# Tail inputs of superblocks 1 to 3 of a deep cross network: by a transposing load and on-chip DMAs in place of TensorE

## The chip, the cores and the metric

The kernel runs on one core of one Trainium2 chip. The metric is the device time of one execution in microseconds; before the change it is 129.14 us, the median of 3 runs (129.04 to 129.23). Profiles are taken in separate executions.

## The reference

Six cross layers over a batch of 4096 rows with 416 features, all in bf16:

```python
B, F, D, L = 4096, 26, 16, 6        # Din = F * D = 416
x = x0                              # [4096, 416]
for l in range(6):
    x = x0 * (x @ ws[l] + bs[l]) + x    # ws[l]: [416, 416]
```

The kernel uses another form of it: with x_l = x0 * s_l and s_0 = 1, s_(l+1) = x_l @ ws[l] + bs[l] + s_l. The products are summed up in PSUM over all layers, and the biases and the 1, summed beforehand, are added where x_l = x0 * s_l is taken out.

## The kernel before

**Tiles.** The batch is cut into four superblocks of 1024 rows (`SB`), each with two halves of 512 (`H`). Activations lie transposed: features on the partitions, batch rows along the free axis. The 416 features are three full chunks of 128 (`CH`) and a tail of 32 features (`DR`). The tail would use 32 partitions only, so it is folded: the superblock's 1024 rows are four groups of 256 (`G`), and group g lies on partitions 32g to 32g+31 (`quad(g)`). For each superblock s, `x0t_sb[:, s, 0, :]` holds the folded tail of x0 and `x0t_sb[:, s, 1, :]` the same with neighbouring quads exchanged (group g^1 on quad g), which `tail_rows` needs so that both halves of a bank can be fed from any quad. The tail of x_l (`xt_sb`) has the same two forms.

**One layer of one superblock.** TensorE does nine `main` steps for half 0 (three output chunks by three input chunks, four matmuls of 32 columns side by side in each), `tail_rows` (the contribution of the 32 tail features), `tail_outs` (the 32 tail outputs, from the full chunks), and nine `main` steps for half 1; every matmul is issued at line 260. VectorE takes each bank out, multiplied with x0 (`leave`, line 412). The tail goes another way: ScalarE adds the bias (`tail_halves`, line 422), GpSimd multiplies with x0's tail (`leave_tail`, line 435), and ScalarE and GpSimd make the exchanged copy (`swap`, lines 399 and 401). Layer l+1 needs that tail only in `tail_rows`, after the nine steps of half 0.

**Where x0's tail comes from.** For superblock 0 a matmul with the identity transposes it in the first layer (`tail_in(0)`), and ScalarE copies it out of PSUM (line 383). For superblocks 1 to 3 all the rows' last 32 columns are loaded in one DMA, `xtl1`, into `xtl_sb`: 24 pieces of 64 bytes per partition, 192 KB. In layer 2 of the superblock before, `tail_in(s+1)` transposes eight tiles of 128 rows on TensorE into the free half of the first tail bank, `keep_tail_in` copies them to `x0t_sb` on ScalarE (line 390), and in layers 3 and 4 ScalarE makes the exchanged copy in four pieces (line 399).

**Order of the work.** `Plan.add` takes the operations in program order for each engine and works out the semaphore waits from what they read and write; nothing is reordered. A DMA is issued by the queue it is added to. On SyncE (SP in the profile) these are, in order: the first rows and weights, `xtl0`, the transposed x0 of half of superblock 0, the weights of layers 1 to 5 with `xtl1` between layer 2's and layer 3's, the three transposing loads of x0's full chunks for superblocks 1 to 3 (`load_transposed`, line 205), the rows `xr` that the end of the kernel needs, and then for each finished superblock four transposing DMAs of the result (`transpose_block`, lines 452 and 457) and, one layer after the next superblock's first, its store (`store_block`, line 469). Plain loads are issued at line 187. The last layer of the last superblock is computed in row form and stored in six pieces (line 666).

Of the kernel before, what the change touches and what calls it, by code (L numbers as in the profile page):

```python
# [8 lines left out]
ACTF = mybir.ActivationFunctionType  # L9
# [109 lines left out]
def bass_standalone__dcn_v2_cross__recsys_kernel(  # L119
# [6 lines left out]
    B, D = x0.shape  # L126
    L = ws.shape[0]
    NC = 3
    DF = 128 * NC
    DR = D - DF  # L130
    assert DR == 32
    SB = 1024
    NS = B // SB
    H = SB // 2
    G = SB // 4
    JS = SB // 128
    NJ = B // 128
    T_BANK = (6, 7)
# [3 lines left out]
    with ExitStack() as es:  # L142

        def sb(name, shape, dt=BF16):
            return es.enter_context(nc.sbuf_tensor(name, shape, dt))
# [2 lines left out]
        wt_sb = sb("wt_sb", [128, L, D])  # L148
        wc_sb = sb("wc_sb", [128, L, 2, 128])
        xin_sb = sb("xin_sb", [128, 4, D])  # L150
        xtl_sb = sb("xtl_sb", [128, NJ, DR])
        xr_sb = sb("xr_sb", [128, JS, D])
        x0T_sb = sb("x0T_sb", [128, NC, B])
        x0t_sb = sb("x0t_sb", [128, NS, 2, G])
# [10 lines left out]
        ident = sb("ident", [128, 128])  # L165
# [6 lines left out]
        ps = es.enter_context(nc.psum_tensor("ps", [128, 8, 512], FP32))  # L172
        psT = ps.bitcast(BF16)

        x0_v = x0.rearrange("(j p) d -> p j d", p=128)
        out_v = out.rearrange("(j p) d -> p j d", p=128)
        P = Plan()

        def quad(q):
            return slice(32 * q, 32 * q + 32)  # L180
# [5 lines left out]
        def load(queue, dst, src, name, writes):  # L186
            P.add(queue, lambda e: e.dma_start(dst, src), writes=writes, dma=name)  # L187

        def load_main(l):
            load(  # L190
                "sync", w_sb[:, l, :, :], ws[l, 0:DF, :].rearrange("(k p) n -> p k n", p=128), "w%d" % l, [("w", l)]
            )

        def load_rows(queue, i):
            load(queue, xin_sb[:, 2 * i:2 * i + 2, :], x0_v[:, 2 * i:2 * i + 2, :], "xin%d" % i, [("xin", i)])
# [7 lines left out]
        def load_transposed(s, a, b):  # L203
            P.add(
                "sync", lambda e: e.dma_start_transpose(x0T_sb[:, :, s * SB + a:s * SB + b], x0[s * SB + a:s * SB + b, 0:DF]),  # L205
                writes=[("x0T", s, c, h) for c in CH for h in HALVES if a <= h * H < b], dma="x0T%d" % s,
            )

        load_rows("sync", 0)
        load_rows("scalar", 1)  # L210
        load_main(0)
# [5 lines left out]
        load_main(1)  # L217
        load_tail_weights(2, L, "wt2", ("sync",) * 4)
        load_main(2)
        load("sync", xtl_sb[:, JS:NJ, :], x0_v[:, JS:NJ, DF:D], "xtl1", [("xtl", 1)])  # L220
        load_main(3)
        load_main(4)
        load_main(5)
        for s in range(1, NS):
            load_transposed(s, 0, SB)
        load("sync", xr_sb[:, :, :], x0_v[:, (NS - 1) * JS:NJ, :], "xr", [("xr",)])


# [3 lines left out]
            reads=[("ones",)], writes=[("dummy",)],  # L232
# [3 lines left out]
                out=ident[:, :], in_=ones_sb[:, 0:128], pattern=[[-1, 128]],  # L236
# [6 lines left out]
                out=u_sb[:, :], in_=ones_sb[0:L + 1, 0:L], pattern=[[1, L]],  # L243
# [34 lines left out]
        def src_main(s, l):  # L278
            if l == 0:
                return x0T_sb, s * SB  # L280
            return xT_sb[:, l % 2], 0
# [77 lines left out]
                adds=[("ps", T_BANK[h]) for h in HALVES],  # L359
            )  # L360

        def tail_in(s):
            def fn(pe):
                for o in range(2 if s == 0 else 1):
                    for r in range(2):
                        for g in range(4):
                            j = 2 * (g ^ o) + r
                            src = xin_sb[:, j, DF:D] if s == 0 and j < 4 else xtl_sb[:, s * JS + j, :]
                            b, c = (7, o * G) if s == 0 else (T_BANK[0], G)
                            ins = mm(  # L370
                                pe, ps[quad(g), b, c + r * 128:c + (r + 1) * 128], src, ident[:, :],
                                s == 0 and o == 0 and r == 0, (0, 32 * g),
                            )
                return ins

            b = 7 if s == 0 else T_BANK[0]
            P.add(
                "tensor", fn, reads=[("ident",), ("xtl", 0 if s == 0 else 1)] + ([("xin", 0), ("xin", 1)] if s == 0 else []),
                adds=[("ps", b)],
            )  # L380
            if s == 0:
                P.add(
                    "scalar", lambda e: e.activation(
                        out=x0t_sb[:, s, :, :], in_=ps[:, 7, :].rearrange("p (o c) -> p o c", o=2), func=ACTF.Copy
                    ), reads=[("ps", 7)], writes=[("x0t", s), ("x0t", s, "swapped")],
                )

        def keep_tail_in(s):
            P.add(
                "scalar", lambda e: e.activation(out=x0t_sb[:, s, 0, :], in_=ps[:, T_BANK[0], G:2 * G], func=ACTF.Copy),  # L390
                reads=[("ps", T_BANK[0])], writes=[("x0t", s)],
            )
        def swap(tile, key, engines):
            for g, eng in enumerate(engines):
                if eng is None:
                    continue
                dst, src = tile[quad(g), 1, :], tile[quad(g ^ 1), 0, :]
                if eng == "scalar":
                    fn = lambda e, d=dst, s=src: e.activation(out=d, in_=s, func=ACTF.Copy)  # L399
                else:  # L400
                    fn = lambda e, d=dst, s=src: e.tensor_copy(out=d, in_=s)  # L401
                P.add(eng, fn, reads=[key], parts=[key + ("swapped",)], shifts=True)
# [74 lines left out]
        for i in range(2):  # L477
            for c in CH:
                b = HEAD_BANKS[i][c]
# [10 lines left out]
                dst, src = x0T_sb[:, c, i * 256:(i + 1) * 256], psT[:, b, 0:256]  # L490
                if c == 1:
                    P.add(
                        "scalar", lambda e, d=dst, s=src: e.activation(out=d, in_=s, func=ACTF.Copy),
                        reads=[("ps", b)], writes=[("x0Tp", c, i)],
                    )
                else:
                    P.add(
                        "vector", lambda e, d=dst, s=src: e.tensor_copy(out=d, in_=s),  # L498
                        reads=[("ps", b)], writes=[("x0Tp", c, i)],
# [28 lines left out]
        for s in range(NS):  # L528
            for l in range(L):
                ending = s == NS - 1 and l == L - 2  # L530
                if s == NS - 1 and l == L - 1:
                    break
                if s == 0 and l == 0:
                    for k in CH:
                        for m in CH:
                            main(s, l, 0, m, k)
                        if k == 0:
                            bias_sums()
                        if k == 1:
                            tail_in(0)  # L540
                    tail_outs(s, l, True)
                    tail_rows(s, l, False)
                    for c in CH:
                        leave(s, l, 0, c)
                else:
                    for m in CH:
                        for k in CH:
                            main(s, l, 0, m, k)
                    tail_rows(s, l, l == 0)
                    for c in CH:  # L550
                        leave(s, l, 0, c)
                    tail_outs(s, l, False)
                if l == 2 and s < NS - 1:
                    tail_in(s + 1)
                leave_tail(s, l, not ending)
                if l == 2 and s < NS - 1:
                    keep_tail_in(s + 1)
                if s == 0 and l == 0:
                    corner(2, L, "wt2")
                if l == 1 and s > 0:  # L560
                    store_block(s - 1)
                if s < NS - 1 and l in (3, 4):
                    g = 2 * (l - 3)
                    swap(x0t_sb[:, s + 1], ("x0t", s + 1), tuple("scalar" if q // 2 == l - 3 else None for q in range(4)))
                if ending:
                    P.add(
                        "gpsimd", lambda e: e.tensor_tensor(
                            out=bt_sb[:, :], in0=cb_sb[:, NC, L - 1:L], in1=cb_sb[:, NC, L - 2:L - 1], op=ALU.subtract
                        ), reads=[("cb",)], writes=[("bt",)],
                    )  # L570
                    P.add(
                        "gpsimd", lambda e, t=t32_sb[:, l % 2, :]: e.tensor_scalar_add(st_sb[:, :], t, bt_sb[:, :]),
                        reads=[("t32", l % 2), ("bt",)], writes=[("st",)],
                    )
                    for c in CH:
                        keep_sum(0, c, "scalar")
                for m in CH:
                    for k in CH:
                        main(s, l, 1, m, k)
                    leave(s, l, 1, m)  # L580
                if ending:
                    for c in CH:
                        keep_sum(1, c, ("scalar", "scalar", "vector")[c])
            if s < NS - 1:
                transpose_block(s)


        s, l = NS - 1, L - 1
        ROW_BANKS = (6, 7, 0, 1, 2, 3, 4, 5)
        src, off = src_main(s, l)  # L590
# [126 lines left out]
```

## Time and profile before

| what | value |
|---|---|
| time, median of 3 runs | 129.14 us |
| time of the profiled execution | 130.38 us |
| its span | 129.1 us |
| TensorE (PE) busy | 124.2 us, 96% |
| VectorE (DVE) busy | 98.5 us, 76% |
| ScalarE (ACT) busy | 50.0 us, 39% |
| GpSimd (POOL) busy | 39.6 us, 31% |
| DMA, SP's queue | 33392 packets, 12.30 MB, 44.3% of 16 engines |
| granted TensorE clock | 1.00 |

The profile is one execution of the kernel, recorded by the hardware. The span runs from the first instruction to the last; the execution's time is a little longer than it. Busy time of an engine is the time in which at least one of its instructions ran; matmuls are pipelined, so PE being busy does not mean that it runs at its best. PEld is the loading of weights into TensorE, which goes on beside the matmuls. "SPq" and "ACTq" are the issuing of DMAs by those engines, and "to landing" is the time from the issue of a DMA to its last semaphore update. An arrow and a name in square brackets say how long the engine stood idle before a group and what ended that. The DMA engines are busy for most of the first 35 us, and in bursts afterwards.

### The profile page before, as it was taken

To read this page: it belongs to the slowest core of one execution; us is meant where nothing else is said; L and a number is where in the kernel's file an instruction comes from. 1 tells how busy PE (TensorE), PEld (TensorE's weight loads), DVE (VectorE), ACT (ScalarE), POOL (GpSimd) and SP (SyncE) were. 2 spreads that over 40 slices of the span, in tenths; PEclk is the share of its full clock that TensorE was granted. 3 is DMA by queue.
4 is the path that set the end of the run, shared out by engine and by line. 5 is a ranking of instruction groups with operands and counts; after the bars stand their busy time and mean duration, and the time that the engine had idled before them with its cause. 6 is when DMAs were issued, how large, how long until landed. Compare 5 with 4: busy or idle time off the path is not lost.

```text
span 129.1 us, 5328 instructions
## 1 busy us (share of the span) xinstructions
PE 124.2 (96%) x2424; PEld 64.5 (50%) x2424; DVE 98.5 (76%) x150; ACT 50.0 (39%) x112; POOL 39.6 (31%) x88
## 2 busy tenths in 40 slices
PE   6997999999999999999999999999999999999991
PEld 4543545545545545545545545455455455455660
DVE  0309588797797797797797797797797797797973
ACT  1525133473523242373422252364422252253920
POOL 6054342242222251241221350340320441440550
PEclk9999999999999999999999999999999999999999
DMA  3969779999809808000009407000009506100017
GB/s 97 280 147 240 86 209 285 172 197 168 259 9 194 68 8 265 7 0 5 0 5 183 86 0 244 25 5 0 5 0 149 120 5 211 58 0 5 0 38 231
DMA packets 34082, 13.12 MB, mean 102 GB/s; under 512 B 25350, under 2 KB 34060, under 8 KB 34060
## 3 DMA queue, kind: packets, MB, share of 16 engines
q1 hardware_dynamic: 33392, 12.30, 44.3%
q10 hardware_dynamic: 668, 0.48, 1.1%
q8 instruction: 19, 0.31, 1.1%
q14 instruction: 3, 0.02, 0.1%
HBM read 4.07 MB, written 3.41 MB: 58 GB/s over the span
## 4 chain that ended last, share of the span: by engine, by line
PE 88%; SPq 5%; DMA 4%; issue 0%; DVE 0%
PE ps L260 88%; DMA w_sb<-in_ws_dram 4%; SPq L187 3%; SPq L205 2%; DVE o_sb L648 0%
## 5 line engine op out<-in xcount | busy, mean ns | idle before, releaser
L412 DVE SCALAR_TENSOR_TENSOR xT_sb<-ps,cb_sb,x0T_sb 128x512 bf16<-128x512 f32 x120 | 80.9, 744 | 20.3 <-PE ps L260 20.3
L260 PE MATMUL ps<-xT_sb,w_sb 128*32 128x512 bf16 (+1 forms) x1596 | 84.6, 364 | 0.7 <-DMA w_sb<-in_ws_dram 0.7
L260 PEld LDWEIGHTS ps<-xT_sb,w_sb 128*32 128x32 bf16 x1596 | 40.7, 97 | 38.1 <-issue 4.0
L422 ACT ACTIVATE t_sb<-ps,cb_sb 64x256 f32<-64x256 f32 x46 | 21.6, 468 | 52.1 <-PE ps L260 51.8
L435 POOL TENSOR_TENSOR xt_sb<-t_sb,x0t_sb 128x256 bf16<-128x256 f32 x20 | 13.4, 672 | 63.5 <-ACT t_sb L422 63.5
L399 ACT ACTIVATE xt_sb<-xt_sb 32x256 bf16<-32x256 bf16 x38 | 15.7, 414 | 15.4 <-POOL xt_sb L435 15.2
L260 PE MATMUL ps<-x0T_sb,w_sb 128*32 128x512 bf16 (+1 forms) x336 | 19.1, 369 | 0.1
L401 POOL COPY xt_sb<-xt_sb 32x256 bf16<-32x256 bf16 x38 | 14.9, 392 | 2.4
L412 DVE SCALAR_TENSOR_TENSOR xo_sb<-ps,cb_sb,x0T_sb 128x512 bf16<-128x512 f32 x18 | 12.1, 744 | 2.5 <-PE ps L260 2.5
L260 PEld LDWEIGHTS ps<-x0T_sb,w_sb 128*32 128x32 bf16 x336 | 8.3, 97 | 8.1 <-issue 0.8
L260 PE MATMUL ps<-xt_sb,wt_sb 32*128 32x512 bf16 (+1 forms) x152 | 11.6, 326 | 0.0
L260 PE MATMUL ps<-xt_sb,wc_sb 32*128 32x256 bf16 x76 | 7.4, 268 | 0.0
L260 PEld LDWEIGHTS ps<-xt_sb,wt_sb 32*128 32x128 bf16 x152 | 2.3, 91 | 8.1 <-DVE xT_sb L412 6.4
L435 POOL TENSOR_TENSOR xot_sb<-t_sb,x0t_sb 128x256 bf16<-128x256 f32 x3 | 2.0, 673 | 9.9 <-ACT t_sb L422 9.9
L260 PE MATMUL ps<-w_sb,xT_sb 128*32 128x416 bf16 (+1 forms) x60 | 5.1, 339 | 0.0
L399 ACT ACTIVATE x0t_sb<-x0t_sb 32x256 bf16<-32x256 bf16 x12 | 4.9, 410 | 0.1
L253 POOL COPY wc_sb<-wt_sb 32x32 bf16<-32x32 bf16 (+1 forms) x12 | 2.8, 232 | 6.5 <-DMA wt_sb<-in_ws_dram 6.0
L648 DVE TENSOR_TENSOR o_sb<-ps,xr_sb 128x416 bf16<-128x416 f32 x6 | 3.4, 588 | 1.3 <-PE ps L260 1.0
L268 PE MATMUL ps<-ones_sb 128*128 128x256 bf16 x12 | 2.9, 419 | 1.2 <-DVE ones_sb L229 1.2
L260 PEld LDWEIGHTS ps<-xt_sb,wc_sb 32*128 32x128 bf16 x76 | 3.9, 93 | 0.3
L498 DVE COPY x0T_sb<-ps 128x256 bf16<-128x256 bf16 x4 | 1.2, 292 | 3.7 <-PE ps L483 3.4
L444 ACT ACTIVATE sS_sb<-ps,cb_sb 128x512 bf16<-128x512 f32 x5 | 3.0, 689 | 0.0
(41 smaller groups left out, 33.7 us busy)
## 6 DMA issues: line engine op xcount, KB each, us to landing
out_dram<-o_sb SPq DMA_DIRECT2D x3, 832.0 KB, 4.2
w_sb<-in_ws_dram SPq DMA_DIRECT2D x6, 312.0 KB, 5.2
xr_sb<-in_x_dram SPq DMA_DIRECT2D x1, 832.0 KB, 5.8
wt_sb<-in_ws_dram SPq DMA_DIRECT2D x4, 104.0 KB, 3.2
out_dram<-o_sb SPq DMA_DIRECT2D x2, 208.0 KB, 2.2
xin_sb<-in_x_dram ACTq DMA_DIRECT2D x1, 208.0 KB, 3.3
xin_sb<-in_x_dram SPq DMA_DIRECT2D x1, 208.0 KB, 3.0
out_dram<-o_sb ACTq DMA_DIRECT2D x2, 104.0 KB, 2.0
```

The source lines that it names most:

```text
L187: P.add(queue, lambda e: e.dma_start(dst, src), writes=writes, dma=name)
L205: "sync", lambda e: e.dma_start_transpose(x0T_sb[:, :, s * SB + a:s * SB + b], x0[s * SB + a:s * SB + b, 0:DF]),
L253: "gpsimd", lambda e, p=p, g=g: e.tensor_copy(out=wc_sb[p, a:b, g % 2, quad(g)], in_=wt_sb[p, a:b, DF:D]), reads=[("wt", name), ("wc", nam ...
L260: return pe.matmul(dst, lhsT=lhsT, rhs=rhs, start=start, stop=True, skip_group_check=True, tile_position=pos,)
L268: ins = pe.matmul(ps[:, 7, 0:256], lhsT=ones_sb[:, 0:128], rhs=ones_sb[:, :], start=True, stop=True)
L399: fn = lambda e, d=dst, s=src: e.activation(out=d, in_=s, func=ACTF.Copy)
L401: fn = lambda e, d=dst, s=src: e.tensor_copy(out=d, in_=s)
L412: "vector", lambda e: e.scalar_tensor_tensor(out=dst, in0=ps[:, bank(h, c), :], scalar=cb_sb[:, c, l:l + 1], in1=x0T_sb[:, c, o:o + H], op ...
L422: "scalar", lambda e, p=p, h=h: e.activation(out=dst[p, :], in_=ps[p, T_BANK[h], 0:G], func=ACTF.Identity, bias=cb_sb[p, NC, l:l + 1]), re ...
L435: "gpsimd", lambda e: e.tensor_tensor(out=dst, in0=t, in1=x0t_sb[:, s, 0, :], op=ALU.mult),
L444: fn = lambda e: e.activation(out=o, in_=i, func=ACTF.Identity, bias=b)
L648: "vector", lambda e: e.tensor_tensor(out=o_sb[:, jj, :], in0=ps[:, b, 0:D], in1=xr_sb[:, j, :], op=ALU.mult), reads=[("ps", b), ("xr",)], ...
```

## The change

`xtl_sb` shrinks to superblock 0, and the `xtl1` load goes. After each of the three `load_transposed(s, 0, SB)`, SP also issues `load_last_columns(s)`: a transposing DMA of the last 128 columns of the superblock's 1024 rows into `tT_sb[:, s - 1, :]`, so that the 32 tail features lie on partitions 96 to 127 and the rows along the free axis. `place_tail(s)` then issues, on SP too, eight DMAs from SBUF to SBUF of 32 partitions by 256 elements: for each of the two forms and each group, from partitions 96 to 127 to the quad where it belongs. They stand where ScalarE's `keep_tail_in` stood, in layer 2 of the superblock before; in SP's order that is behind `xr` for superblock 1, and behind the store of the last finished superblock for 2 and 3. `tail_in` is left for superblock 0 alone, `keep_tail_in` and the four swaps of `x0t_sb` in layers 3 and 4 are gone. `tail_rows` of layer 0 and `leave_tail` now wait for those DMAs.

```diff
-        xtl_sb = sb("xtl_sb", [128, NJ, DR])
+        xtl_sb = sb("xtl_sb", [128, JS, DR])
+        tT_sb = sb("tT_sb", [128, NS - 1, SB])
...
+        def load_last_columns(s):
+            P.add(
+                "sync", lambda e: e.dma_start_transpose(tT_sb[:, s - 1, :], x0[s * SB:(s + 1) * SB, D - 128:D]),
+                writes=[("tT", s)], dma="tT%d" % s,
+            )
+
+        def place_tail(s):
+            for o in range(2):
+                for g in range(4):
+                    dst, src = x0t_sb[quad(g), s, o, :], tT_sb[128 - DR:128, s - 1, (g ^ o) * G:((g ^ o) + 1) * G]
+                    P.add(
+                        "sync", lambda e, d=dst, r=src: e.dma_start(d, r), reads=[("tT", s)],
+                        writes=[("x0t", s), ("x0t", s, "swapped")], dma="x0t%d" % s,
+                    )
...
         load_main(2)
-        load("sync", xtl_sb[:, JS:NJ, :], x0_v[:, JS:NJ, DF:D], "xtl1", [("xtl", 1)])
         load_main(3)
         load_main(4)
         load_main(5)
         for s in range(1, NS):
             load_transposed(s, 0, SB)
+            load_last_columns(s)
         load("sync", xr_sb[:, :, :], x0_v[:, (NS - 1) * JS:NJ, :], "xr", [("xr",)])
...
-        def tail_in(s):
+        def tail_in():
             def fn(pe):
-                for o in range(2 if s == 0 else 1):
+                for o in range(2):
                     for r in range(2):
                         for g in range(4):
                             j = 2 * (g ^ o) + r
-                            src = xin_sb[:, j, DF:D] if s == 0 and j < 4 else xtl_sb[:, s * JS + j, :]
-                            b, c = (7, o * G) if s == 0 else (T_BANK[0], G)
+                            src = xin_sb[:, j, DF:D] if j < 4 else xtl_sb[:, j, :]
...
-        def keep_tail_in(s):
-            P.add(
-                "scalar", lambda e: e.activation(out=x0t_sb[:, s, 0, :], in_=ps[:, T_BANK[0], G:2 * G], func=ACTF.Copy),
-                reads=[("ps", T_BANK[0])], writes=[("x0t", s)],
-            )
...
-                if l == 2 and s < NS - 1:
-                    tail_in(s + 1)
                 leave_tail(s, l, not ending)
                 if l == 2 and s < NS - 1:
-                    keep_tail_in(s + 1)
+                    place_tail(s + 1)
...
-                if s < NS - 1 and l in (3, 4):
-                    g = 2 * (l - 3)
-                    swap(x0t_sb[:, s + 1], ("x0t", s + 1), tuple("scalar" if q // 2 == l - 3 else None for q in range(4)))
```

More of the change, by code (lines that the diff above doesn't have):

```diff
@@ L367, in fn @@
                             j = 2 * (g ^ o) + r
-                            src = xin_sb[:, j, DF:D] if s == 0 and j < 4 else xtl_sb[:, s * JS + j, :]
-                            b, c = (7, o * G) if s == 0 else (T_BANK[0], G)
+                            src = xin_sb[:, j, DF:D] if j < 4 else xtl_sb[:, j, :]
                             ins = mm(
-                                pe, ps[quad(g), b, c + r * 128:c + (r + 1) * 128], src, ident[:, :],
-                                s == 0 and o == 0 and r == 0, (0, 32 * g),
+                                pe, ps[quad(g), 7, o * G + r * 128:o * G + (r + 1) * 128], src, ident[:, :],
+                                o == 0 and r == 0, (0, 32 * g),
                             )
                 return ins
-            b = 7 if s == 0 else T_BANK[0]
+            P.add("tensor", fn, reads=[("ident",), ("xtl", 0), ("xin", 0), ("xin", 1)], adds=[("ps", 7)])
             P.add(
-                "tensor", fn, reads=[("ident",), ("xtl", 0 if s == 0 else 1)] + ([("xin", 0), ("xin", 1)] if s == 0 else []),
-                adds=[("ps", b)],
-            )
-            if s == 0:
-                P.add(
[L383 to L386, printed above, removed]
-        def keep_tail_in(s):
-            P.add(
-                "scalar", lambda e: e.activation(out=x0t_sb[:, s, 0, :], in_=ps[:, T_BANK[0], G:2 * G], func=ACTF.Copy),
-                reads=[("ps", T_BANK[0])], writes=[("x0t", s)],
+                "scalar", lambda e: e.activation(
+                    out=x0t_sb[:, 0, :, :], in_=ps[:, 7, :].rearrange("p (o c) -> p o c", o=2), func=ACTF.Copy
+                ), reads=[("ps", 7)], writes=[("x0t", 0), ("x0t", 0, "swapped")],
             )
@@ L539, in bass_standalone__dcn_v2_cross__recsys_kernel @@
                         if k == 1:
-                            tail_in(0)
+                            tail_in()
                     tail_outs(s, l, True)
```

## The prediction

> **What bounds the kernel now.** I read the page first, then the chain that ended last in order of time, then busy time by stretches cut at the layers, then SP's queue and the DMA table.
>
> From the page:
>
> ```profile
> span 129.1 us, 5328 instructions
> PE 124.2 (96%) x2424; PEld 64.5 (50%) x2424; DVE 98.5 (76%) x150; ACT 50.0 (39%) x112; POOL 39.6 (31%) x88
> ...
> PE 88%; SPq 5%; DMA 4%; issue 0%; DVE 0%
> ```
>
> The chain in order of time:
>
> ```profile
> 7.29 5.14 DMA w_sb<-in_ws_dram
> 12.43 0.04 issue
> 12.47 114.02 PE ps L260 x2184
> 126.49 0.02 issue
> 126.52 0.59 DVE o_sb L648
> ```
>
> From 12.47 us the chain is PE alone, without a break. Before that it is SP's issues and the load of the weights of layer 1. So PE work taken out between 12.47 and 126.49 shortens the run one for one, and anything else counts only if it makes PE wait.
>
> Stretches from one layer's tail_rows to the next (columns: stretch, its length, then busy us and instructions of PE, PEld, DVE, ACT, POOL, the clock, DMA share, GB/s). Superblocks 0, 1, 2; layer 2 and then layer 3 of each:
>
> ```profile
> 19.41:24.40 4.99, 4.99 (x109) 2.59 (x106) 4.04 (x6) 2.15 (x5) 1.45 (x3) 1.00 1.16 228
> 24.40:29.28 4.88, 4.88 (x102) 2.48 (x98) 4.04 (x6) 2.60 (x6) 1.45 (x3) 1.00 1.00 210
> 48.79:53.78 4.99, 4.99 (x109) 2.59 (x106) 4.05 (x6) 2.15 (x5) 1.46 (x3) 1.00 0.53 172
> 53.78:58.66 4.88, 4.88 (x102) 2.48 (x98) 4.04 (x6) 2.60 (x6) 1.45 (x3) 1.00 0.01 3
> 78.17:83.16 4.99, 4.99 (x109) 2.59 (x106) 4.04 (x6) 2.15 (x5) 1.46 (x3) 1.00 0.53 174
> 83.16:88.04 4.88, 4.88 (x102) 2.48 (x98) 4.04 (x6) 2.60 (x6) 1.45 (x3) 1.00 0.01 3
> ```
>
> A layer with the tail input in it is 0.11 us longer, three times alike, with DVE equally busy (4.04 of 4.99 or 4.88, so DVE is not the bound) and the clock at 1.00.
>
> The timeline inside the first of them, the place in superblock 1 that needs the tail, SP's queue, and four rows of DMA issues:
>
> ```profile
> 20.30 0.28 PE L260 MATMUL ps<-ident,xtl_sb 128*32 128x128 bf16 x8
> 23.30 0.38 ACT L390 ACTIVATE x0t_sb<-ps 128x256 bf16<-128x256 f32 x1
> ...
> 39.03 0.12 PEld L260 LDWEIGHTS ps<-x0t_sb,wt_sb 32*128 32x128 bf16 x8 [0.42 <-DVE xo_sb L412]
> ```
> ```profile
> 10.19 1.57 SPq L187 DMA_DIRECT2D xtl_sb<-in_x_dram  x1
> 11.80 5.89 SPq L187 DMA_DIRECT2D w_sb<-in_ws_dram  x3
> 17.74 11.63 SPq L205 DMA_TRANSPOSE x0T_sb<-in_x_dram  x3
> 29.42 0.59 SPq L187 DMA_DIRECT2D xr_sb<-in_x_dram  x1
> 37.37 4.12 SPq L452 DMA_TRANSPOSE o_sb<-xo_sb  x3
> ```
> ```profile
> xr_sb<-in_x_dram SPq DMA_DIRECT2D x1, 832.0 KB, 5.8
> wt_sb<-in_ws_dram SPq DMA_DIRECT2D x6, 26.0 KB, 2.2
> o_sb<-xo_sb SPq DMA_TRANSPOSE x9, 3.3
> ot_sb<-xot_sb SPq DMA_TRANSPOSE x3, 2.4
> ```
>
> The reader is to see 39.03 us: today's tail of superblock 1 is there by 33.7 (the last swap, 32.87 + 0.82), five us early. In the changed kernel it comes through SP's queue, behind everything of the second and third fence.
>
> **The change part by part.**
>
> *Off PE: 3 x 8 matmuls of 128 columns.* By the stretches: 4.99 - 4.88 = 0.11 each, 0.33 in all, on the path. It fits the single records: the eight start between 20.30 and 20.36 and the next matmul at 20.41. [...]
>
> *Off ACT: 3 copies of 0.38 and 12 swaps of 0.41 (4.9 by the page), 6.0 us of busy time.* Worth nothing: behind them ACT waits 1.8, 1.4 and 1.6 us for PE in the three layers of superblock 0 concerned. Were that cover gone, up to 0.85 a layer would come back as gain; no row asks for it. leave_tail of layer 2 no longer waits for the eight matmuls, 0.1 earlier; POOL then waits some 3 us for ACT in every layer anyhow.
>
> *Off SP and the DMA engines: the xtl1 load,* 1.57 us of SP at 10.19. The chain's load (w1) was issued at 7.29, ahead of it, so the 12.43 should stay; w3 to w5 come earlier and nobody waits for them. Bounds for w1: 0 to a gain of 0.66, PE's whole idle time there; I take 0. In the three weight issues behind it (5.89 us where 0.43 apiece is normal) up to 5.89 - 3 x 0.43 = 4.6 us of SP time may be freed too.
>
> *Onto SP: three transposing loads of 256 KB.* Nearest rows: o_sb transposes of the same 128 x 1024 took 4.12 / 3 = 1.37 of SP each; a third of an x0T load is 11.63 / 9 = 1.29. Three: 3.9 to 4.1 us. All stand before xr.
>
> *Onto SP: 8 placing DMAs of 16 KB per superblock.* Nearest row by size and partitions: the 26 KB wt loads, 0.42 to 0.57 of SP and 2.2 us to landing. 8 x 0.47 = 3.8 us. The first waits for its transposing load; queued behind it on SP are transpose_block and store_block. That load is issued about 20 us and, landing as late as the worst x0T (7.4 us), is there by 28, before SP comes to it.
>
> *When is the tail of superblock 1 there?* SP ends xr today at 30.01. Without xtl1, with three more loads, then the eight: 30.01 - 1.57 + 4.0 + 3.8 = 36.2 at the latest; 31.6 if all 4.6 us are freed; I take 34, in the middle, as the stall of the weight issues follows the slow xtl1 rows but not surely all of it. From the end of the last issue to landing 2.2 - 0.47 = 1.7: 33.3 to 37.9, middle 35.7. The DMA engines give a second bound, as the placing stands behind xr in one queue. xr lands at 29.42 + 5.8 = 35.2. Three loads by DMA time: 768 KB took about 3.8 us of the stretch that starts at 17.74, so 3 x 1.3 = 3.8 more; xtl1 occupied the engines from 12.4 to about 15.3 (88 GB/s there), 2.9 less; the eight add some 0.6. So 36.7, and 39.6 if the freed 2.9 us goes unused. I take 36.7. Needed at 39.03 - 0.11 = 38.9: 2.2 us to spare, 0.7 late at worst. Cost taken 0; ends 0 and 0.7.
>
> [...] The four 26 KB loads issued from 5.29 to 7.25 landed 2.0 us after their issues at the median, so they overlapped; I go by them.)
>
> *Superblocks 2 and 3.* The placing stands behind the out stores, at 48.5 and 77.9, ends 4 us later on a queue otherwise idle to 66.75 and 96.13, and is needed at about 68 and 97.5. Nothing.
>
> *The output transposes of block 0* need SP at 37.4; SP is free by 36.2 at the latest. Their cover if late: ot_sb lands at about 45.6, POOL copies it at 47.70: 2.1 us.
>
> *New waits on PE,* three times for a DMA semaphore in tail_rows of layer 0. Not shown before in that place; PEld's gap there is 0.42 whichever semaphore ended it. Bounds 0 and 0.1 each (a quarter of that gap); I take 0.
>
> **Sum.** -0.33 + 0 + 0. The profiled execution took 130.38, 1.28 more than its span; the unprofiled median is 129.14 and the PE stretches should be the same in it. 129.14 - 0.33 = 128.8, a span of 128.8 too. That is 0.26%; about 0.2% (0.26 us) is what a measurement can tell from no change here, so the forecast is just over it.
>
> **The rivals.**
>
> *The tail of superblock 1 comes late (slower).* Place: tail_rows of layer 0, superblock 1. For it: eight DMAs at the end of a queue that is full up to 35.2 today. Against: the 2.2 us. It decides from a landing after 38.9; at 39.26 the gain is gone, at 39.5 it is measurably slower. By the worst bound (39.6) it is 129.14 - 0.33 + 0.7 = 129.5; with one of the long pauses that the transposes had (ot_sb 4.0 against 2.3 us, another 1.7), 131.2.
>
> *The gain is eaten by waits (same).* Three PE waits at 0.1 each leave 0.03: 129.1. Against it: 4.88 us for layers that wait for ACT, DVE or POOL alike.
>
> *More than PE's part (faster).* w1 earlier without the xtl1 descriptors in the rings: at most 0.66 more, 128.15. Against it: xtl1 is issued 2.9 us after w1, behind it in each ring.
>
> **How the numbers follow.** No stall 0.71 (128.8, own range 128.65 to 129.0, the spread of the three times to both sides); late tail 0.19 (129.0 to 131); waits 0.06 (129.1); more 0.04. Faster by over 0.2%: four fifths of the first (its centre is close to the bound) and the last, 0.61. Same: the rest of the first (0.14), the waits and the mild end of the late tail (0.03), 0.23. Slower: the rest of the late tail, 0.16. The range runs from 128.6, below the likeliest by the spread, to 129.5, the worst landing by the bounds; about 0.05 lies below it and 0.1 above.
>
> **What would show it.** Layer 2 of superblocks 0 to 2 at 4.88; L390 and the x0t_sb form of L399 gone; xr issued between 27.7 and 32.5; the eight placing issues ending between 31.6 and 36.2; PE's chain 113.7 us from 12.47. Wrong, if PE or PEld waits for a DMA on x0t_sb near 39, if the w1 row moves, or if a placing DMA takes SP well over 0.5 us.

## The result

The changed kernel is slower: 134.73 us median of 6 executions (131.90 to 136.30) against 129.18 us (128.95 to 129.27). The ratio is 1.026, 95% interval 1.021 to 1.030, but it leaves out executions over 1.5% above the fastest, which here are the changed kernel's own long stalls, so the median belongs beside it. On another chip it took 134.12 to 136.16 us in four executions (ratio 1.042, 1.036 to 1.048). The forecast was 128.8, in a range of 128.6 to 129.5.

### The profile after

The page of the changed kernel, from an execution of 135.76 us (the line PEclk is the granted clock in tenths, in 40 slices):

```profile
span 134.5 us, 5290 instructions
PE 126.7 (94%) x2400; PEld 65.1 (48%) x2400; DVE 98.7 (73%) x150; ACT 44.3 (33%) x97; POOL 39.7 (29%) x88
...
PEclk9999999999995599999999999999999999999999
...
PE 67%; SPq 27%; DMA 2%; issue 1%; DVE 0%
```

PE's share of the chain fell from 88% to 67%: the chain no longer joins PE at 12.47. Its end, in order of time:

```profile
38.45 2.70 DMA x0t_sb<-tT_sb
41.15 0.14 issue
41.29 90.10 PE ps L276 x1664
131.39 0.02 issue
131.41 0.59 DVE o_sb L648
```

It runs through SP's queue up to the last of the eight placing DMAs of superblock 1, which lands at 41.15. In the timeline PE waits for it:

```profile
41.26 0.27 PEld L276 LDWEIGHTS ps<-x0t_sb,wt_sb 32*128 32x128 bf16 x8 [3.67 <-issue]
41.29 1.01 PE L276 MATMUL ps<-x0t_sb,wt_sb 32*128 32x512 bf16 x7 [3.21 <-DMA x0t_sb<-tT_sb]
```

The layers by stretches, in the columns of the prediction: layer 2 of superblock 0, then the last layer of superblock 0 with the stall at its end, the first of superblock 1, and the two next, of which the last is again a layer 2:

```profile
18.50:23.38 4.88, 4.88 (x101) 2.48 (x98) 4.04 (x6) 1.77 (x4) 1.46 (x3) 1.00 1.31 170
33.13:41.29 8.16, 4.95 (x101) 2.52 (x98) 4.04 (x6) 0.94 (x2) 0.67 (x1) 0.95 0.71 175
41.29:49.03 7.74, 7.74 (x97) 3.37 (x98) 4.32 (x6) 1.77 (x4) 1.45 (x3) 0.61 0.46 88
49.03:53.91 4.88, 4.88 (x101) 2.48 (x98) 4.04 (x6) 1.77 (x4) 1.85 (x4) 1.00 0.02 3
53.91:58.78 4.87, 4.87 (x100) 2.47 (x96) 4.04 (x6) 1.77 (x4) 1.46 (x3) 1.00 0.62 194
```

The reader is to see three things. Layer 2 is 4.88 and 4.87, the saving that was forecast. The layer before the tail's arrival is 8.16, 3.28 more than a layer. And the layer after it is 7.74 with PE busy throughout and the clock at 0.61: PE came back from the stall at half speed (a clock of 0.50 from 40.43 to 47.25). From the two rows, the time at half clock is 2 x (0.05 x 8.16 + 0.39 x 7.74) = 6.85 us.

SP's queue:

```profile
12.54 4.79 SPq L206 DMA_TRANSPOSE x0T_sb<-in_x_dram  x1
17.38 2.33 SPq L212 DMA_TRANSPOSE tT_sb<-in_x_dram  x1
19.75 5.53 SPq L206 DMA_TRANSPOSE x0T_sb<-in_x_dram  x1
25.32 1.30 SPq L212 DMA_TRANSPOSE tT_sb<-in_x_dram  x1
26.66 4.41 SPq L206 DMA_TRANSPOSE x0T_sb<-in_x_dram  x1
31.12 1.31 SPq L212 DMA_TRANSPOSE tT_sb<-in_x_dram  x1
32.47 0.58 SPq L188 DMA_DIRECT2D xr_sb<-in_x_dram  x1
33.10 5.95 SPq L221 DMA_DIRECT2D x0t_sb<-tT_sb  x8
39.09 4.06 SPq L457 DMA_TRANSPOSE o_sb<-xo_sb  x3
```

The two spans differ by 5.34 us (134.47 - 129.13): stall +3.28, half clock 7.74 - 4.88 = +2.86, three shorter layers -0.33, layer 1's weights, late in the execution shown of before and not here, -0.9 with the head, and the end of the kernel +0.4. That last one, which the prediction has nowhere, is read from the end of the chain: from 131.41 + 0.59 = 132.0 to the span's end it is 2.5 us, before it was 129.1 - 127.1 = 2.0.

### The profile page after: what moved, and what is told of

Read it like the earlier page. It is cut to its first block, busy times and chain, and to the rows that moved or that the text cites. A ratio compares the mean times of both kernels' runs of the same rounds, so it can differ in the third digit from the quotient of the medians.

```text
span 134.5 us, 5290 instructions
## 1 busy us (share of the span) xinstructions
PE 126.7 (94%) x2400; PEld 65.1 (48%) x2400; DVE 98.7 (73%) x150; ACT 44.3 (33%) x97; POOL 39.7 (29%) x88
## 3 DMA queue, kind: packets, MB, share of 16 engines
HBM read 3.87 MB, written 3.41 MB: 54 GB/s over the span
## 4 chain that ended last, share of the span: by engine, by line
PE 67%; SPq 27%; DMA 2%; issue 1%; DVE 0%
PE ps L276 67%; SPq L206 12%; SPq L188 7%; SPq L221 4%; SPq L212 4%; DMA x0t_sb<-tT_sb 2%; DVE o_sb L648 0%
## 5 line engine op out<-in xcount | busy, mean ns | idle before, releaser
L276 PE MATMUL ps<-x0T_sb,w_sb 128*32 128x512 bf16 (+1 forms) x336 | 21.4, 401 | 0.1
L404 ACT ACTIVATE xt_sb<-xt_sb 32x256 bf16<-32x256 bf16 x38 | 15.7, 414 | 15.5 <-POOL xt_sb L440 15.3
L276 PEld LDWEIGHTS ps<-x0T_sb,w_sb 128*32 128x32 bf16 x336 | 8.9, 104 | 9.6 <-issue 2.9
L276 PE MATMUL ps<-xt_sb,wt_sb 32*128 32x512 bf16 (+1 forms) x152 | 11.6, 326 | 0.0
L276 PE MATMUL ps<-x0t_sb,wt_sb 32*128 32x512 bf16 (+1 forms) x32 | 2.9, 371 | 3.2 <-DMA x0t_sb<-tT_sb 3.2
```

The costliest lines, as they stand in the source:

```text
L276: return pe.matmul(dst, lhsT=lhsT, rhs=rhs, start=start, stop=True, skip_group_check=True, tile_position=pos,)
```

## The experiments

Three questions: is the place in SP's queue the cause of the late tail; is the half clock the stall's doing; and what is left when both are gone. All edits are against the changed kernel unless it is said otherwise.

### Early placing of superblock 1

```diff
             load_transposed(s, 0, SB)
+            if s == 2:
+                place_tail(1)
             load_last_columns(s)
...
-                if l == 2 and s < NS - 1:
+                if l == 2 and 0 < s < NS - 1:
                     place_tail(s + 1)
```

> The changed kernel with the eight placing DMAs of superblock 1 issued right behind the second x0T load, ahead of two transposing loads, the third x0T load and xr. Theory (place in SP's queue): the tail landed at 41.15 because SP came to the first placing DMA at 33.10; here SP comes to it at about 25, the tail lands by 33, no stall at 37.7 and no halved clock: 3.3 + 2.9 us come back, about 128 to 128.9. Rival (the placing DMAs are slow by themselves or choke on the transposing loads around them): 0.6 to 1.2 us of SP each and a late last engine here too, landing after 38.8, a stall of 1 us or more and over 130.

129.96 us against 129.50; ratio 1.0033 (1.0009 to 1.0058). SP's queue and the two layers around the old stall, from its timeline and stretches:

```profile
24.71 5.86 SPq L221 DMA_DIRECT2D x0t_sb<-tT_sb  x8
```
```profile
33.42:38.30 4.88, 4.88 (x101) 2.48 (x98) 4.04 (x6) 0.94 (x2) 0.67 (x1) 1.00 1.16 182
38.30:43.18 4.88, 4.88 (x102) 2.48 (x98) 4.04 (x6) 1.77 (x4) 1.46 (x3) 1.00 1.42 266
```

Stall and half clock are gone, although the eight issues take as long as before (5.86 us). So the place in the queue decides. But the kernel is no faster than before. The 0.33 us of the layers is there: the unbroken last stretch of PE's chain is 116.63 us, against 116.95 in both profiles below that have the old way of the tail and no wait for layer 1's weights. It is given back elsewhere. The chain ends at 126.15 and its span is 128.6, 2.45 us later: the longer end is in this kernel too. The two make +0.1 us; the median is 0.46 higher, and the interval reaches down to +0.12. What the rest of the 0.46 is, no profile shows.

### The xr load behind the placing

```diff
-        load("sync", xr_sb[:, :, :], x0_v[:, (NS - 1) * JS:NJ, :], "xr", [("xr",)])
...
                     place_tail(s + 1)
+                    if s == 0:
+                        load("sync", xr_sb[:, :, :], x0_v[:, (NS - 1) * JS:NJ, :], "xr", [("xr",)])
```

> The changed kernel with the xr load issued behind the eight placing DMAs of superblock 1 in place of ahead of them. It asks which part of the queue in front makes the tail late. If each us in front counts: SP's 0.63 and the 2.4 us of DMA time of xr leave the front, the tail lands 0.6 to 2.5 earlier (38.6 to 40.5 against 41.15), the stall shrinks to 1 to 2.8 us, the clock stays whole, 130 to 132. If the placing DMAs' own pace sets the landing (0.59 us each and 2.7 us behind the last issue), only SP's 0.63 comes back and the stall stays near 2.7. If xr alone was the cause, no stall, 129.3.

130.76 us against 129.40; ratio 1.0087 (1.0060 to 1.0114). From its timeline:

```profile
32.20 5.66 SPq L221 DMA_DIRECT2D x0t_sb<-tT_sb  x8
...
39.16 0.59 PE L275 MATMUL ps<-x0t_sb,wt_sb 32*128 32x512 bf16 x7 [0.79 <-DMA x0t_sb<-tT_sb]
```

The issues end at 37.86, 1.2 us earlier than in the changed kernel, and the first matmul waits until 39.16, 1.3 us later; in the changed kernel these are 39.05 and 41.29, 2.2 apart (1.9 and 2.9 in the two other profiles below with xr ahead). So xr cost twice: on SP, where its issue takes 0.58 of the 1.2, and in the time of the placing DMAs from issue to landing, 3.2 us at the median behind xr in the changed kernel and 2.1 ahead of it here. This run doesn't divide the remaining 0.79 us of standing between the three transposing loads, which still stand in front, and the eight issues themselves. The clock stays whole.

### Matmuls on constants in the stall

```diff
+                    if s == 1 and l == 0:
+                        fill(24)
                     tail_rows(s, l, l == 0)
```

`fill(n)` issues n matmuls on a tile of ones, and nobody reads what they write.

> The changed kernel with 24 matmuls on constants (128 x 256, some 2.6 us) on TensorE ahead of the first tail_rows of superblock 1, that is within the stall. They write a free part of a bank and nothing is made of them. Theory (the half clock from 41.3 to 46.9 follows from TensorE standing still for over 3 us): idle time falls below 1 us in a run with the stall of the profile, the clock stays at 1.00, 131.5 to 132.5 and a much smaller spread between runs. Rival (the transposing DMAs of block 0 at 39 to 45, or the waiting itself, slow TensorE): the layer of 7.74 us stays, 134 to 135.

132.75 us (131.95 to 133.10) against 129.50; ratio 1.0247 (1.0211 to 1.0283). The layer with the stall and the one after, and the first matmul behind the wait, from its stretches and its timeline:

```profile
32.84:41.23 8.39, 7.67 (x124) 4.77 (x121) 4.04 (x6) 0.94 (x2) 0.67 (x1) 1.00 0.71 176
41.23:46.11 4.88, 4.88 (x96) 2.49 (x97) 4.04 (x6) 1.77 (x4) 1.46 (x3) 1.00 1.00 119
```
```profile
41.23 0.59 PE L276 MATMUL ps<-x0t_sb,wt_sb 32*128 32x512 bf16 x7 [0.72 <-DMA x0t_sb<-tT_sb]
```

The tail comes as late as ever, but PE stands for 0.72 us only, and the layer of 7.74 is 4.88, beside the same transposing DMAs. The half clock is the standstill's doing, not that of the DMAs, beside which the clock is 1.00 here.

With 12 such matmuls:

> The changed kernel with 12 constant matmuls (1.3 us) in the stall, half as many as in the run with 24. The clock halved after a standstill of 3.59 us (two windows of 3.41) and of 2.72 (one window), and stayed whole after 1.17 and 0.99. Here TensorE stands about 1.5 to 2.3 us. If the limit lies near 3 us the clock stays whole and the time is 132 to 133; if it lies near 2 us some runs show a window at half clock (mean clock 0.987) and 1.7 us more.

(The lengths in this expectation, 3.59, 2.72, 1.17 and 0.99, count from the start of the last matmul before the gap; from its end they are the 3.21, 2.35, 0.79 and 0.72 of this text. Its windows are the stretches at half clock in the profiles, 6.83 us after 3.21 of standing and 3.41 after 2.35.) Two executions took 132.52 and 130.63 us, both with a mean clock of 1.00. The third, which was profiled, took 185.75 us with the clock at 0.65 from its first layers on; why is not known. It shows nothing of the gap, and how the clock takes a standstill between 0.79 and 2.35 us stays open.

### The changed kernel again

> The changed kernel once more, beside the others on one chip. Theory (stall of varying length at the tail of superblock 1, and half the clock afterwards when it is long): 131.9 to 136.3 again, with the stall in the profile longer than 3 us where the mean clock is below 0.99, and shorter where it is 1.0.

135.61 us (134.12 to 136.16). Its stall in the timeline and the layer after it:

```profile
40.83 0.59 PE L276 MATMUL ps<-x0t_sb,wt_sb 32*128 32x512 bf16 x7 [2.35 <-DMA x0t_sb<-tT_sb]
```
```profile
40.83:47.39 6.56, 6.56 (x96) 3.02 (x96) 4.32 (x6) 1.77 (x4) 1.46 (x3) 0.74 0.90 114
```

2.35 us of standing cost 2 x 0.26 x 6.56 = 3.4 us at half clock, and the layer 1.68; 3.21 us of standing cost twice as much time at half clock, 6.8 us, and the layer 2.86. The expectation that only stalls over 3 us do it was wrong. Finer stretches show when the clock changed, first in the profile with 3.21 us of standing, then in this one:

```profile
38.08:40.43 2.35, 0.00 (x0) 0.00 (x0) 0.00 (x0) 0.00 (x0) 0.00 (x0) 1.00 0.18 47
40.43:43.84 3.41, 2.55 (x36) 1.43 (x40) 1.88 (x3) 0.69 (x2) 0.00 (x0) 0.50 1.01 195
43.84:47.25 3.41, 3.41 (x40) 1.30 (x36) 1.95 (x4) 1.08 (x3) 1.45 (x3) 0.50 0.32 60
```
```profile
40.83:41.57 0.74, 0.74 (x20) 0.52 (x24) 0.28 (x1) 0.00 (x0) 0.00 (x0) 1.00 1.01 181
41.57:44.98 3.41, 3.41 (x44) 1.50 (x40) 2.83 (x5) 1.77 (x4) 1.46 (x3) 0.50 1.23 121
```

In the one the clock fell while PE still stood, in the other 0.74 us after it had started again; in both PE had stood for 2.35 of the 3.41 us before. The ten executions of this kernel fit the same steps: a mean clock of 0.975 (6.8 us at half) in five of 135.29 to 136.30 us, 0.987 (3.4 us) in three of 133.81 to 135.93, and 0.998 or 1.000 in the two shortest, 131.90 and 132.66. A standstill of 2.35 us was enough for a stretch of 3.41 us at half clock.

### The kernel before with xtl1 behind the weights

```diff
-        load("sync", xtl_sb[:, JS:NJ, :], x0_v[:, JS:NJ, DF:D], "xtl1", [("xtl", 1)])
         load_main(3)
         load_main(4)
         load_main(5)
+        load("sync", xtl_sb[:, JS:NJ, :], x0_v[:, JS:NJ, DF:D], "xtl1", [("xtl", 1)])
```

> The kernel before with the xtl1 load moved behind the weights of layer 5, nothing else. Theory (xtl1's small descriptors are behind the late last engine of layer 1's weights, 12.43 us before and 10.53 changed): those weights land near 10.5, layer 1 starts 0.9 us earlier, 128.2. Rival (the late engine is the instruction fetch at 10.2 us, in the profiled execution alone or by chance of its place): 129.0 to 129.3 as before.

129.50 us against 129.50; ratio 1.0010 (0.9992 to 1.0027). Layer 1's weights are in time in this profile, but the median doesn't move, so the place of the xtl1 load costs nothing that can be seen. The weights are in time in the profile of the run with more DMAs on SP too, where xtl1 stands in its old place: the late weights of the profile of before came with that execution, whose 130.38 us is above every other of that kernel on record.

### Superblock 1 through TensorE, 2 and 3 by DMA

```diff
-        xtl_sb = sb("xtl_sb", [128, JS, DR])
+        xtl_sb = sb("xtl_sb", [128, 2 * JS, DR])
...
         load_main(2)
+        load("sync", xtl_sb[:, JS:2 * JS, :], x0_v[:, JS:2 * JS, DF:D], "xtl1", [("xtl", 1)])
...
-            load_last_columns(s)
+            if s > 1:
+                load_last_columns(s)
...
+                if l == 2 and s == 0:
+                    tail_in(1)
                 leave_tail(s, l, not ending)
-                if l == 2 and s < NS - 1:
+                if l == 2 and s == 0:
+                    keep_tail_in(1)
+                elif l == 2 and s < NS - 1:
                     place_tail(s + 1)
```

with the old `tail_in`, `keep_tail_in` and swaps for superblock 1.

> The change for superblocks 2 and 3 alone: superblock 1 keeps its way through TensorE, with an xtl1 load of 8 pieces of 64 bytes per partition in place of 24. Theory: no wait for the tail anywhere, two of three savings of 0.11 us: 128.9, and less if smaller xtl1 also helps the head. Rival (the new path costs in superblocks 2 and 3 too, by its waits or by DMA traffic): 129.2 or more, and layers of superblocks 2 and 3 longer than 4.88 us.

129.14 us against 129.50; ratio 0.9986 (0.9966 to 1.0006). No stall, every layer of superblocks 2 and 3 at 4.88, and the short end: its chain ends at 125.87, its span is 127.9. The size is that of two savings (0.22 us are 0.17%), but the interval reaches 1, so a gain is not shown.

### More DMAs on SP, and nothing else

The kernel before, with

```diff
+        more_sb = sb("more_sb", [128, 25, 256])
...
+                if l == 2 and s == 3:
+                    P.add("sync", None, reads=[("more", n) for n in range(25)])
+                if l == 2 and s in (1, 2):
+                    for i in range(11 + s):
+                        n = 12 * (s - 1) + i
+                        dst = more_sb[quad(i % 4), n, :]
+                        src = w_sb[96:128, 0, 0, 0:256] if i < 6 else ws[0, DF:D, 0:256]
+                        P.add(
+                            "sync", lambda e, d=dst, r=src: e.dma_start(d, r), reads=[("w", 0)],
+                            writes=[("more", n)], dma="more%d" % s,
+                        )
```

> The kernel before with 25 more DMAs on SP, 12 in layer 2 of superblock 1 and 13 of superblock 2, of 32 partitions by 256 elements into a tile that nobody reads, half of them from SBUF and half from HBM; SP waits for them in superblock 3. SP has then 80 instructions as in the changed kernel, and nothing on TensorE depends on them. Theory (length of SP's stream): the gap of 0.46 us before SP's last wait appears, +0.4 us, ratio 1.003. Rival: 1.000. And the issue: 0.59 us each from SBUF; from HBM 0.42 to 0.47 as the 26 KB weight loads if the source is what makes the placing DMAs slower to issue, 0.59 as well if it is something else.

130.16 us against 129.40; ratio 1.0040 (1.0014 to 1.0067). The end of its chain, its span, and the issues of the tile (durations are min/median/max in ns):

```profile
span 129.0 us, 5354 instructions
```
```profile
125.89 0.59 DVE o_sb L660
```
```profile
L571 SPq DMA_DIRECT2D more_sb<-in_ws_dram x13: 412/423/1456, 52.7 to 86.2; - x13
L571 SPq DMA_DIRECT2D more_sb<-w_sb x12: 590/593/1395, 47.9 to 82.0; - x12
```

From 126.48 to 129.0 it is 2.5 us again. So DMAs that were issued 40 us earlier or more, and that SP waits for in superblock 3 and nothing at the end, make the end longer (2.5 us in place of 2.0): that was the give-back of the early placing, as far as it is found. And a DMA of this shape costs SP 0.42 us from HBM and 0.59 from SBUF.

### The placing of superblock 3 on ScalarE

On top of the early placing:

```diff
-                if l == 2 and 0 < s < NS - 1:
-                    place_tail(s + 1)
+                if l == 2 and s == 1:
+                    place_tail(2)
+                if l >= 2 and s == 2:
+                    place_tail(3, "scalar", (2 * l - 4, 2 * l - 3))
```

where `place_tail` takes the queue, and which of the eight it issues.

> The kernel with the early placing DMAs of superblock 1, and with the eight of superblock 3 issued by ScalarE, two after each layer's tail in layers 2 to 5 of superblock 2, in place of SP. SP's stream is eight instructions shorter (72 as in the mixed kernel, against 80). Theory (with 80 instructions SP crosses into a further block of its stream just before its last wait, and its fetch holds up the end by 0.4 us, which ate the 0.33 that TensorE saved): the gap before the last wait is gone, 128.9 to 129.2 beside a before of 129.5, ratio 0.997 to 0.998. Rival (early placing costs something else, in the head or by DMA traffic): 129.9 again, ratio 1.003.

129.22 us against 129.40; ratio 0.9977 (0.9953 to 1.0002).

> The version with the early placing DMAs of superblock 1 and those of superblock 3 on ScalarE once more, unchanged, to narrow its interval (0.9953 to 1.0002). Theory (three savings of 0.11 us and nothing given back): ratio 0.997 to 0.998. Rival: 1.000.

129.42 us against 129.39; ratio 1.0002 (0.9977 to 1.0027). In both profiles all layers are at 4.88 and the end is 2.0 us (chain 125.88 and span 127.9; 126.29 and 128.3). From the first layer on they are 0.33 us shorter than the old way (116.62 and 116.63 us of PE against 116.95); what differs between the two is the head, where the first tail_rows came at 9.09 and at 9.49 us. That head varies by more than the saving, in the kernel before too (its executions here lie from 128.95 to 130.33). So the version gives back nothing that can be seen, but that it is faster is not shown.

## Why the prediction was wrong

**The saving on PE** was right: 4.99 became 4.88, three times, and nothing came of ACT's 6.0 us. **New waits on PE** and **superblocks 2 and 3** at nothing were right too: with the early placing every layer is 4.88. **w1** at nothing was right by the run that moved xtl1; but the 5.14 us from w1's issue to its landing in the profile of before were an exception, and with w1 in time PE needed the tail at 33.13 + 4.88 = 38.0, not at 38.9. The prediction read that time from an execution whose head was 0.9 us late.

**When the tail of superblock 1 is there** is the step that failed. The prediction took 35.7 to 36.7 and at worst 39.6; it was 41.15. By its terms:

| term | taken | bounds given | measured |
|---|---|---|---|
| start of the first x0T load on SP, from 17.74 | 13.9 | 11.6 to 16.2 | 12.54 |
| three x0T and three tT issues | 15.6 | 15.5 to 15.7 | 14.7 + 4.9 = 19.7 |
| xr issued | 30.2 | to 32.4 | 33.05 |
| eight placing issues | 3.8 | none | 5.95 |
| last issue to landing | 2.2 | none | 2.7 |

(The first row's bounds and value are the step's own: 1.57 us of xtl1, and 0 to 4.6 freed in the weight issues.) SP got more time back than was taken for it (1.4 us), and lost three times that in the transposing loads (4.1 us). The nearest rows were right for an undisturbed load: tT took 1.30 and 1.31 against 1.29 to 1.37 taken, and with early placing one x0T took 3.58 against 11.63 / 3 = 3.88. The other four took 2.33, 4.79, 5.53 and 4.41, and three 16 KB fetches of instructions, at 17.0, 23.0 and 28.6 us, fell in with them. In the first stretch here, during the first tT load,

```profile
17.40:19.70 2.30, 2.30 (x56) 1.21 (x52) 1.47 (x4) 0.09 (x1) 0.01 (x1) 1.00 1.21 106
```

the DMA engines are fully taken at 106 GB/s, where the stretches of the two undisturbed tT issues show 290. Over all profiles the x0T loads of superblocks 2 and 3 took 3.46 to 3.69 us without a fetch (7 loads) and 3.96 to 5.53 with one (17). The x0T load of superblock 1 is another matter: it is issued right behind the weights of layers 2 to 5, and it took 5.28 to 5.56 us in three profiles in which no fetch fell in with it. So a fetch is not needed for its 4.79, and what makes it long is not shown. Rows of before showed such a hold-up as well (2.16 us for one ot_sb transpose against 1.24; x0T 4.16 against 3.65), but no term was made of it.

For the placing issues the nearest row was chosen by size and partitions. Its source was HBM, and that was the wrong kinship: 0.59 from SBUF, 0.42 from HBM for one shape. Eight of them make 1.3 us of the 2.15 missed (8 x 0.63 with the gaps, against 8 x 0.47), the rest is held-up issues, one of 1.24 us.

**The rival of a late tail** had the right place and mechanism, with 0.19 of the chance. Its price left out the clock, which was at half for 6.8 us around 3.21 us of standing. By its own landing it would be 3.28 us of stall; the half clock added 2.86, and the time jumps between executions with the number of stretches of 3.41 us at half clock. Only the most pessimistic figure in it (131.2) is near the measured 131.9 to 136.3.

**The length of SP's program** was no term at all. +0.44 us at the end (2.47 from the last VectorE instruction, against 2.03) outweighs the whole saving of 0.33, so the change would have been no gain without the stall either, as the early placing shows (1.0009 to 1.0058).

## What to carry to other kernels

A transfer that moves from a late producer on the chip to a queue must be costed with everything ahead of it in that queue, at the pace of its disturbed rows too, and against the earliest time that its reader can need it; the cure is its place in the queue, here 8.4 us earlier. A stall of TensorE such as the 2.35 and 3.21 us here is not priced by its length alone, but with the time at half clock as well (1.7 and 2.9 us more). And a saving of 0.3 us in a kernel's middle is smaller than what the longer issuing program cost at the end here, 0.44 us: look at the distance from the last compute to the span's end too.

## What the runs showed of the hardware that was not expected

- SP's DMA issue of 32 partitions by 512 bytes took 0.59 us with the source in SBUF and 0.42 with it in HBM (medians of 12 and 13 issues).
- With 80 instructions on SP in the trace the span ends 2.44 to 2.50 us after the last VectorE instruction (six profiles; 2.29 in the one with the clock at 0.65), with 54 or 72 it ends 2.02 to 2.04 us after it (five profiles). In the profile of the changed kernel a packet of 8 KB on an instruction queue follows some 0.6 us after the span's end, and none in that of before. The crossing into a further block of SP's stream, whose fetch holds up the end, was the author's theory in the run with the placing on ScalarE; only the dependence on the number was shown, and the instructions that differ are nearly all DMA issues, so that the number of DMAs on SP is not told apart.
- The clock halved for 6.8 us around a standstill of TensorE of 3.21 us, for 3.4 us after one of 2.35, and not at all after 0.79 and 0.72.
- A transposing load whose issue falls in with a 16 KB fetch of instructions took longer on SP: tT 2.23 to 2.35 us in six such cases against 1.30 or 1.31 in the others, among which one was reached by a fetch in its last 0.11 us only. The fetch itself was not moved by an experiment, and it is not the only such cause: without one, transposes of the output took 2.0 to 2.6 us against some 1.3 in the four kernels that issue the placing early or xr late.
